# The convolution's last step moved into the slots of the last two attention units

## The chip, the cores and the metric

The kernel runs on one core of one Trainium2 chip. The metric is the device time of one execution in microseconds. The kernel before took 1053.49 us, the median of three runs (1046.73 to 1053.63).

## The reference

Two sequence mixers run over the same input `u` (2048 rows, 448 columns), and a gate per row joins them.

```
g = sigmoid((u * gate_w).sum(-1))
K = 2 * real(einsum("dn,dnl->dl", C, exp(A * dt * l)))     # a kernel of 2048 taps for each column
a = irfft(rfft(u, 4096) * rfft(K, 4096))[:2048] + u * D_skip
q, k, v = u @ wq, u @ wk, u @ wv                            # 16 heads of 28, 4 segments of 512 rows
for s in range(4):
    a_dot = causal_softmax(qs @ ks.T * 28**-0.5) @ vs
    a_mem = phi(qs) @ M / (phi(qs) @ z + 1e-6)              # memory of the segments before
    o     = sigmoid(beta) * a_mem + (1 - sigmoid(beta)) * a_dot
    M, z  = M + phi(ks).T @ vs, z + phi(ks).sum()
b = concat(o) @ wo
out = g * a + (1 - g) * b
```

## The kernel before

The first part, to about 560 us, projects q, k, v, transforms `u` for the convolution and builds the taps; it leaves its results in DRAM. The change is in the second part, `second_half`.

That part goes through 16 attention units: `i = 4 * segment + head group`, four heads in each. A unit has six slots (`r`). In a slot stand one step of the row maxima two units ahead (`maxima`), one step of this unit's scores and exponentials (`weigh`), and, spread between, steps of two other chains: the convolution `cv` (`convolve`: 82 steps, `RATIO` = 1.1 of them a slot from unit 1 on) and the ends of segments (`ends`). The product with the values of a unit (`values`) follows in slot 1 of the next unit.

`seg_end(s)` ends a segment. `norm` takes the denominators out of `pvs` through DRAM (tile `dn`), inverts them, brings them back as `r8` (`r` in the trace), spreads them over the partitions with a matmul by `sel`, and scales `pvs`. Then four output tiles follow: `out_mm` multiplies by `wo`, `store` adds the skip term `u * D_skip * g` and writes the tile to the DRAM buffer `TB`. Then `recall(s + 1)` loads the memory's numerators `am`, inverts their denominators and scales them. Each of these uses the one PSUM buffer `ps_m`; scores, convolution and last step share three buffers `ps_a`.

The convolution's spectrum goes to the DRAM buffer `BB`. When `cv` has ended, with unit 13, its SBUF pool is closed and `finish` begins. It has eight column groups `wc`, each of 64 x 2 x 2 rows of the output. `load` fetches a group of `BB` (tile `bt`), `early` and `late` fetch the group of `TB` (tile `rest`), and `last` makes the inverse transform with four matmuls, multiplies it by the gate and adds it to `rest` on DVE, and stores the result. The rows of a group are spread over the whole sequence, so each group needs rows of all segments: `early` brings the rows of segments 0 to 2 (48 of 64 partitions of each half), `late` those of segment 3.

Segment 3 is ended by `norm(3, 0, 3)` for three head groups and `last_end` for the fourth: it writes four tiles to `TB`, and only then `late` and all eight `last` can run:

```
    k.last_end()
    load_b(6)
    for wc in range(8):
        late(wc)
    for wc in range(8):
        last(wc)
        if wc == 0:
            load_b(7)
```

Engines run their instructions in program order, as a scheduler in the building step put them; so a DMA that waits for a buffer holds up every DMA behind it on the same queue (SP's, ACT's or POOL's). A DMA queue's semaphores are reused after eight issues.

Of the kernel before, what the change touches and what calls it, by code (L numbers as in the profile page):

```python
# [22 lines left out]
D = 448  # L23
# [395 lines left out]
class Feed:  # L419
# [146 lines left out]
def finish(nc, k, fp):  # L566


    bv = k.BB.rearrange("k r (h w) d -> h (k r) w d", h=2)
    ov = k.out.rearrange("(n h w) d -> h n w d", h=2, w=16)  # L570
    tv = k.TB.rearrange("(n h w) d -> h n w d", h=2, w=16)
    bts, rest = {}, {}

    def load(wc):
        for h in range(2):
            bts[wc, h] = fp.tile([128, 2, D], F32, tag="bt", name="bt", bufs=14)
            k.dma(bts[wc, h], bv[h, :, 2 * wc : 2 * wc + 2])

    def early(wc):

        rest[wc] = k.spare(wc)
        for h in range(2):
            k.dma(rest[wc][64 * h : 64 * h + 48], tv[h, :48, 2 * wc : 2 * wc + 2])

    def late(wc):
        for h in range(2):
            k.adma(rest[wc][64 * h + 48 : 64 * h + 64], tv[h, 48:, 2 * wc : 2 * wc + 2])

    def last(wc):
        ws = slice(2 * wc, 2 * wc + 2)  # L590
        py = k.ps("a")
        for w in range(2):
            for h in range(2):
                k.mm(
                    py[64 * h : 64 * h + 64, w, :D], k.fc, bts[wc, h][:, w],
                    start=True, stop=True, tile_position=(0, 64 * h),
                )
        yo = rest[wc]
        for w in range(2):
            i = 2 * wc + w  # L600
            nc.vector.scalar_tensor_tensor(yo[:, w], py[:, w, :D], k.gt2[:, i : i + 1], yo[:, w], ALU.mult, ALU.add)
        for h in range(2):
            k.dma(ov[h, :, ws], yo[64 * h : 64 * h + 64])

    return load, early, late, last

# [198 lines left out]
def attend(nc, k, ap):  # L805
# [177 lines left out]
    def store(s, t, po, xt):  # L983
        i = 4 * s + t
        tb = ap.tile([128, D], F32, tag="tb", name="tb", bufs=2)
        nc.scalar.activation(tb, po, AF.Copy, scale=k.ogt[:, i : i + 1])  # L986
        v.scalar_tensor_tensor(tb, xt, k.gt[:, i : i + 1], tb, ALU.mult, ALU.add)
        (k.adma if s == 3 else k.dma)(k.TB[128 * i : 128 * i + 128], tb)

    def out_mm(s, t, po, hgs):  # L990
        for hg in hgs:
# [4 lines left out]

    def seg_end(s):
        yield from norm(s, 0, 4, k.pdma)
        for t in range(4):
            xt = skip(s, t)  # L1000
            po = k.ps("m")
            out_mm(s, t, po[:, :D], range(4))
            store(s, t, po[:, :D], xt)
            yield
        yield from recall(s + 1)

    def last_end():

        s = 3
        end = norm(s, 3, 4, k.adma)  # L1010
        next(end)
        xts = [skip(s, t) for t in range(4)]
        pos = [k.ps("a") for _ in range(2)]
        for t in range(4):
            out_mm(s, t, pos[t // 2][:, t % 2, :D], range(3))
        for _ in end:
            pass
        for t in range(4):
            po = pos[t // 2][:, t % 2, :D]
            out_mm(s, t, po, [3])  # L1020
            store(s, t, po, xts[t])

    def spare(wc):

        t = ap.tile([128, 2, SEG], F32R, tag="qk"[wc % 2], name="rest", bufs=4)
        return t[:, :, :D].bitcast(F32)

    k.load, k.maxima, k.weigh, k.values, k.seg_end = load, maxima, weigh, values, seg_end
    k.norm, k.last_end, k.spare = norm, last_end, spare


def second_half(nc, k, ap, tp, fp, fin):

    none = object()

    def step(g):
        return next(g, none) is not none

    nothing = iter(())
    attend(nc, k, ap)
    k.load(0)
# [12 lines left out]
    nc.vector.tensor_copy(g16, pm[:16, :128])  # L1056
    k.dma(k.GD.rearrange("(i p) -> i p", p=128), g16)
    k.gt2 = ap.tile([128, 16], F32, name="gt2")
    for h in range(2):
        k.dma(k.gt2[64 * h : 64 * h + 64], k.GD.rearrange("(n h w) -> h n w", h=2, w=16)[h])  # L1060
    fp = fp()
    cv = convolve(nc, k, fp)
    for r in range(3):
        step(ms[1])
    step(ms[0])
    step(ms[0])
    for r in range(3):
        step(ms[1])
    ends = []
    acc = 0.0  # L1070
    vals = nothing
    fi = None
    n = 0
    for i in range(16):
        k.load(i + 3)
        ahead = ms.get(i + 2, nothing)
        behind = ms.get(i + 1, nothing)
        w = k.weigh(i)
        for r in range(6):
            step(ahead)  # L1080
            step(w)
            if r == 0:
                step(behind)
            if r == 1:
                step(vals)
                step(behind)
                if i % 4 == 0 and i > 0:
                    ends.append(k.seg_end(i // 4 - 1))
                if i == 15:
                    ends.append(k.norm(3, 0, 3, k.pdma))  # L1090
            elif ends and not step(ends[0]):
                ends.pop(0)
                if ends:
                    step(ends[0])
            if i >= 1 and fi is None:
                acc += RATIO
# [38 lines left out]
def gated_mix(ctx, tc, k):  # L1135
# [172 lines left out]
```

## Time and profile before

| | before |
|---|---|
| time, median of 3 runs | 1053.49 us (1046.73 to 1053.63) |
| the profiled execution | 1054.63 us, span 1052.8 us |
| mean granted TensorE clock | 0.818 |
| PE busy | 793.4 us (75%) |
| DVE, ACT, POOL busy | 558.5, 559.0, 160.6 us |
| DMA | 151.35 MB, mean 144 GB/s |

The span is the time from the first instruction to the last in one execution that the hardware profiler recorded. PE is TensorE, PEld its weight loads, DVE VectorE, ACT ScalarE, POOL GpSimd; SPq, ACTq and POOLq are DMA issues on the queue of that engine. A row of the timeline has the start, the time it takes, engine, line, operation, output and inputs, count, and in brackets the idle time before it with what ended it. The chain of work that ended last has the start, the duration and what the time went to. In a fp32 product each matmul of the program is two or more records.

### The profile page before, as it was taken

The numbers are of one execution on the slowest core, as the hardware profiler recorded it, in microseconds if no ns is written. First come the engines' busy times: TensorE is split into PE (matmuls) and PEld (weight loads), VectorE is DVE, ScalarE is ACT, GpSimd is POOL, SyncE is SP. The second block draws the span as 40 slices with busy tenths as digits, with TensorE's granted clock in tenths as the row PEclk, the third lists the DMA queues.
The fourth block names the chain that finished last, engine by engine and source line by source line (L and its number), as shares of the span: only waits on it lengthen the run. The fifth ranks groups of instructions, "written<-read, shape, count | busy, mean of one in ns | idle before, by whom it ended". The sixth has DMA issues, their size and how long they took to land.

```text
span 1052.8 us, 18763 instructions
## 1 busy us (share of the span) xinstructions
PE 793.4 (75%) x7413; PEld 440.2 (42%) x7413; DVE 558.5 (53%) x1115; ACT 559.0 (53%) x669; POOL 160.6 (15%) x215
## 2 busy tenths in 40 slices
PE   1265677798777798759975268998999899987485
PEld 0152434355444565437642134444444444444231
DVE  6491524346666476775664045555557555571133
ACT  3425556668888688888883123454335344432210
POOL 0401010101111110101110101113122213222300
PEclk9775776779888899879996565798799789888687
DMA  7853252534222234210624944357446555318607
GB/s 203 247 157 97 83 166 74 167 110 142 82 91 91 90 122 137 86 59 28 190 79 150 348 186 152 96 170 232 131 137 215 177 179 189 127 45 330 137 29 218
DMA packets 90858, 151.35 MB, mean 144 GB/s; under 512 B 20619, under 2 KB 60931, under 8 KB 90723
## 3 DMA queue, kind: packets, MB, share of 16 engines
q1 hardware_dynamic: 80818, 130.26, 39.3%
q10 hardware_dynamic: 8480, 18.62, 4.8%
q0 software_dynamic: 1472, 1.27, 0.5%
q8 instruction: 58, 0.95, 0.4%
q14 instruction: 30, 0.24, 0.1%
HBM read 89.95 MB, written 59.78 MB: 142 GB/s over the span
## 4 chain that ended last, share of the span: by engine, by line
PE 45%; DVE 17%; DMA 14%; ACT 12%; issue 7%; SPq 2%; POOL 1%; DVEq 0%; ACTq 0%; POOLq 0%
PE ps_m L1146 18%; PE ps_a L1146 17%; ACT cs L1139 4%; PE ps_pv L1146 4%; DVE jk L851 4%; DVE X L361 4%; PE ps_arg L1146 3%; DVE Y L365 2%; PE ps_k L1146 2%; PE ps_m L1149 2%; DVE Y L366 2%; DMA dm<-DM 2%; ACT EX L1139 2%; DMA dn<-pvs 2%; ACT L1139 1%
## 5 line engine op out<-in xcount | busy, mean ns | idle before, releaser
L851 DVE CUSTOM_DVE_ANT_0 jk<-ps_a,mk 128x512 f32<-128x512 f32 (+3 forms) x256 | 125.0, 488 | 55.1 <-PE ps_a L1146 47.9
L882 ACT ACTIVATE PT<-ps_a 128x1024 f32<-128x1024 f32 (+1 forms) x96 | 84.1, 881 | 94.7 <-PE ps_a L1146 91.3
L327 POOL TENSOR_TENSOR EX<-EX,cab 128x1024 f32<-128x1024 f32 x28 | 53.5, 1912 | 436.0 <-ACT EX L1139 436.0
L1139 ACT ACTIVATE cs<-ps_arg 128x1024 f32<-128x1024 f32 x112 | 108.3, 1020 | 17.2 <-PE ps_arg L1146 15.4
L1146 PE MATMUL ps_m<-xh,w 112*128 112x512 f32 x256 | 101.7, 443 | 11.4 <-DMA w<-WD 7.5
L1146 PE MATMUL ps_k<-Y,X 128*32 128x64 f32 x3584 | 72.1, 242 | 38.8 <-DVE Y L366 38.4
L1146 PE MATMUL ps_a<-qu,ku 32*128 32x384 f32 (+3 forms) x768 | 90.2, 360 | 6.1 <-DVE mx L851 4.7
L361 DVE TENSOR_TENSOR X<-EX,cs 128x1024 f32<-128x1024 f32 x56 | 68.5, 1223 | 40.1 <-ACT cs L1139 28.6
L1146 PEld LDWEIGHTS ps_k<-Y,X 128*32 128x32 f32 x3584 | 62.1, 124 | 60.2 <-DVE Y L366 48.3
L1146 PEld LDWEIGHTS ps_a<-qu,ku 32*128 32x128 f32 x768 | 69.6, 213 | 17.0 <-DVE mx L851 8.8
L1139 ACT ACTIVATE EY<-ps_arg 128x1024 f32<-128x1024 f32 x56 | 56.4, 1029 | 33.9 <-PE ps_arg L1146 33.7
L893 POOL TENSOR_SCALAR_AFFINE_SELECT PT<-PT 128x256 f32<-128x256 f32 (+1 forms) x96 | 46.5, 488 | 165.4 <-ACT PT L882 163.4
L1146 PE MATMUL ps_a<-ku,qu 32*128 32x512 f32 (+3 forms) x256 | 53.8, 464 | 22.9 <-DVE mx L851 21.8
L1146 PEld LDWEIGHTS ps_m<-xh,w 112*128 112x128 f32 x256 | 51.9, 203 | 40.2 <-issue 14.4
L365 DVE TENSOR_TENSOR Y<-EY,cs 128x1024 f32<-128x1024 f32 x56 | 68.3, 1220 | 0.0
L1139 ACT ACTIVATE cs<-cs,bhp 128x1024 f32<-128x1024 f32 x56 | 64.4, 1150 | 1.8
L1146 PEld LDWEIGHTS ps_a<-ku,qu 32*128 32x128 f32 x256 | 25.6, 216 | 89.4 <-DVE mx L851 44.6
L367 DVE SCALAR_TENSOR_TENSOR Y<-EY,cs 128x512 f32<-128x512 f32 x56 | 38.5, 689 | 39.5 <-ACT cs L1139 39.4
L1146 PE MATMUL ps_arg<-ct,lh 48*128 48x512 bf16 x224 | 48.1, 426 | 9.1 <-ACT cs L1139 7.0
L1146 PE MATMUL ps_m<-xl,w 112*128 112x512 f32 x128 | 53.6, 418 | 0.0
L1146 PEld LDWEIGHTS <-lh 48*128 48x128 bf16 x392 | 21.6, 98 | 70.0 <-issue 46.8
L1146 PE MATMUL ps_m<-wo,pvs 128*128 128x448 f32 x96 | 45.6, 625 | 5.9 <-ACT tb L986 4.9
(182 smaller groups left out, 1350.2 us busy)
## 6 DMA issues: line engine op xcount, KB each, us to landing
w<-WD SPq DMA_DIRECT2D x32, 448.0 KB
qu<-QD SPq DMA_DIRECT2D x16, 512.0 KB
ku<-KD SPq DMA_DIRECT2D x16, 512.0 KB
GU<-gs SPq DMA_DIRECT2D x32, 224.0 KB
GK<-gs ACTq DMA_DIRECT2D x8, 896.0 KB
gk<-GK SPq DMA_DIRECT2D x32, 224.0 KB
gu<-GU SPq DMA_DIRECT2D x32, 224.0 KB
BB<-bs ACTq DMA_DIRECT2D x16, 448.0 KB
```

The lines of the kernel that those rows point to most:

```text
L327: nc.gpsimd.tensor_tensor(o, o, cab, ALU.mult)
L361: v.tensor_tensor(X, ex, t[:, :, 0], ALU.mult)
L365: v.tensor_tensor(Y[:, :, :, :32], lo, y[:, :, :, ::-1], ALU.mult)
L366: v.tensor_tensor(Y[:, 0, :, 32:], ey[:, :, 32:], y[:, 0], ALU.mult)
L367: v.scalar_tensor_tensor(Y[:, 1, :, 32:], ey[:, :, 32:], -1.0, y[:, 1], ALU.mult, ALU.mult)
L851: v.tensor_tensor_reduce(junk[:, :n], pt[:, x, o : o + n], k.mk[:, SEG - n :], 1.0, -3e38, ALU.add, ALU.max, mx[:, 3 - t, h : h + 1],)
L882: nc.scalar.activation(PT[:, 2 * hp : 2 * hp + 2, 512 * b : 512 * b + n], pt[:, :, :n], AF.Exp, scale=SCALE)
L893: nc.gpsimd.affine_select(sl, sl, pat, ALU.is_ge, 0.0, base=0, channel_multiplier=-1)
L1139: return tc.keep_in_program_order(nc.scalar.activation(*args, **kw))
L1146: tc.keep_in_program_order(nc.tensor.matmul(*args, **kw))
L1149: tc.keep_in_program_order(nc.tensor.transpose(*args))
```

## The change

- `cv` ends with unit 12: its ratio goes from 1.1 to 1.15 steps a slot. `finish` begins there.
- The segment ends get on faster: a step in slot 0 and slots 2 to 5 as before, but in unit 13 two steps in every slot; and the first steps of `recall` go along with the output tiles. Segment 2 thus ends within unit 13.
- `skip_last`, in slot 2 of unit 11, writes the skip term of segment 3 (`u * D_skip * g`) to `TB`, so that `TB` is complete without the attention of segment 3.
- `load` fetches both halves of a group in one DMA (four buffers of 896 KB instead of fourteen of 448 KB); `join` replaces `early` and `late` and fetches the rows of all four segments in two DMAs of 64 partitions, into six buffers.
- `last` runs in slots: groups 0 to 3 in slots 2 to 5 of unit 14, groups 4 to 7 in slots 0 to 3 of unit 15. It stores the rows of segments 0 to 2 to the output, and those of segment 3 to a new DRAM buffer `YD`.
- `last_end` loads the four tiles of `YD`, adds `(1 - g)` times its attention output in one DVE instruction a tile, and writes segment 3 to the output, alternately on SP's and ACT's queue.

```diff
 def finish(nc, k, fp):
-    bv = k.BB.rearrange("k r (h w) d -> h (k r) w d", h=2)
+    bv = k.BB.rearrange("k r (h w) d -> (k r) h w d", h=2)
     ov = k.out.rearrange("(n h w) d -> h n w d", h=2, w=16)
     tv = k.TB.rearrange("(n h w) d -> h n w d", h=2, w=16)
+    yv = k.YD.rearrange("(n h w) d -> h n w d", h=2, w=16)
     def load(wc):
-        for h in range(2):
-            bts[wc, h] = fp.tile([128, 2, D], F32, tag="bt", name="bt", bufs=14)
-            k.dma(bts[wc, h], bv[h, :, 2 * wc : 2 * wc + 2])
-    def early(wc):
-        rest[wc] = k.spare(wc)
-        for h in range(2):
-            k.dma(rest[wc][64 * h : 64 * h + 48], tv[h, :48, 2 * wc : 2 * wc + 2])
-    def late(wc):
-        for h in range(2):
-            k.adma(rest[wc][64 * h + 48 : 64 * h + 64], tv[h, 48:, 2 * wc : 2 * wc + 2])
+        bts[wc] = fp.tile([128, 2, 2, D], F32, tag="bt", name="bt", bufs=4)
+        k.dma(bts[wc], bv[:, :, 2 * wc : 2 * wc + 2])
+    def join(wc):
+        rest[wc] = fp.tile([128, 2, D], F32, tag="rest", name="rest", bufs=6)
+        for h in range(2):
+            k.dma(rest[wc][64 * h : 64 * h + 64], tv[h, :, 2 * wc : 2 * wc + 2])
     def last(wc):
...
-                    py[64 * h : 64 * h + 64, w, :D], k.fc, bts[wc, h][:, w],
+                    py[64 * h : 64 * h + 64, w, :D], k.fc, bts[wc][:, h, w],
...
         for h in range(2):
-            k.dma(ov[h, :, ws], yo[64 * h : 64 * h + 64])
+            k.dma(yv[h, :, ws], yo[64 * h + 48 : 64 * h + 64])
+        for h in range(2):
+            k.dma(ov[h, :48, ws], yo[64 * h : 64 * h + 48])
 def attend(nc, k, ap):
...
-        (k.adma if s == 3 else k.dma)(k.TB[128 * i : 128 * i + 128], tb)
+        k.dma(k.TB[128 * i : 128 * i + 128], tb)
+    def skip_last():
+        for t in range(4):
+            xt = skip(3, t)
+            i = 12 + t
+            v.tensor_scalar(xt, xt, k.gt[:, i : i + 1], None, ALU.mult)
+            k.dma(k.TB[128 * i : 128 * i + 128], xt)
     def seg_end(s):
         yield from norm(s, 0, 4, k.pdma)
+        memory = recall(s + 1)
         for t in range(4):
...
+            next(memory)
             yield
-        yield from recall(s + 1)
+        yield from memory
     def last_end():
...
-        xts = [skip(s, t) for t in range(4)]
+        yds = []
+        for t in range(4):
+            yd = ap.tile([128, D], F32, tag="xt", name="yd", bufs=4)
+            k.dma(yd, k.YD[128 * t : 128 * t + 128])
+            yds.append(yd)
...
         for t in range(4):
-            po = pos[t // 2][:, t % 2, :D]
+            po, yd, i = pos[t // 2][:, t % 2, :D], yds[t], 12 + t
             out_mm(s, t, po, [3])
-            store(s, t, po, xts[t])
+            v.scalar_tensor_tensor(yd, po, k.ogt[:, i : i + 1], yd, ALU.mult, ALU.add)
+            (k.dma, k.adma)[t % 2](k.out[128 * i : 128 * i + 128], yd)
 def second_half(nc, k, ap, tp, fp, fin):
...
-            elif ends and not step(ends[0]):
-                ends.pop(0)
-                if ends:
-                    step(ends[0])
-            if i >= 1 and fi is None:
+            if r != 1 or i == 13:
+                for _ in range(2 if i == 13 else 1):
+                    while ends and not step(ends[0]):
+                        ends.pop(0)
+            if 1 <= i <= 12:
                 acc += RATIO
...
-            if fi is not None and r % 2 == 1:
-                load_b(n)
+            if i == 11 and r == 2:
+                k.skip_last()
+            if i == 13 and r < 4:
+                load_b(r)
+            if i == 14 and r >= 2 or i == 15 and r < 4:
+                last(n)
+                if n < 2:
+                    join(n + 6)
+                if n < 4:
+                    load_b(n + 4)
                 n += 1
...
-        if i == 13:
+        if i == 12:
             for _ in cv:
                 pass
-            fi = fin()
-            load_b, early, late, last = finish(nc, k, fi)
-        if i == 14:
+            load_b, join, last = finish(nc, k, fin())
+        if i == 13:
             for wc in range(6):
-                early(wc)
+                join(wc)
...
-    early(6)
-    early(7)
     step(vals)
     k.last_end()
-    load_b(6)
-    for wc in range(8):
-        late(wc)
-    for wc in range(8):
-        last(wc)
-        if wc == 0:
-            load_b(7)
-RATIO = 1.1
+RATIO = 1.15
...
+    k.YD = dr.tile([SEG, D], F32, name="YD")
```

More of the change, by code (lines that the diff above doesn't have):

```diff
@@ L594, in last @@
                 k.mm(
-                    py[64 * h : 64 * h + 64, w, :D], k.fc, bts[wc, h][:, w],
+                    py[64 * h : 64 * h + 64, w, :D], k.fc, bts[wc][:, h, w],
                     start=True, stop=True, tile_position=(0, 64 * h),
                 )
-        yo = rest[wc]
+        yo = rest.pop(wc)
         for w in range(2):
@@ L602, in last @@
         for h in range(2):
-            k.dma(ov[h, :, ws], yo[64 * h : 64 * h + 64])
-    return load, early, late, last
+            k.dma(yv[h, :, ws], yo[64 * h + 48 : 64 * h + 64])
+        for h in range(2):
+            k.dma(ov[h, :48, ws], yo[64 * h : 64 * h + 48])
+    return load, join, last
 def project(nc, k, pp):
@@ L1018, in last_end @@
         for t in range(4):
-            po = pos[t // 2][:, t % 2, :D]
+            po, yd, i = pos[t // 2][:, t % 2, :D], yds[t], 12 + t
             out_mm(s, t, po, [3])
-            store(s, t, po, xts[t])
-    def spare(wc):
-        t = ap.tile([128, 2, SEG], F32R, tag="qk"[wc % 2], name="rest", bufs=4)
-        return t[:, :, :D].bitcast(F32)
+            v.scalar_tensor_tensor(yd, po, k.ogt[:, i : i + 1], yd, ALU.mult, ALU.add)
+            (k.dma, k.adma)[t % 2](k.out[128 * i : 128 * i + 128], yd)
     k.load, k.maxima, k.weigh, k.values, k.seg_end = load, maxima, weigh, values, seg_end
-    k.norm, k.last_end, k.spare = norm, last_end, spare
+    k.norm, k.last_end, k.skip_last = norm, last_end, skip_last
 def second_half(nc, k, ap, tp, fp, fin):
@@ L1071, in second_half @@
     vals = nothing
-    fi = None
     n = 0
```

## The prediction

> **What bounds the kernel now.** I read the page first, then the busy time by stage, then the chain of work that ended last.
>
> ```profile
> span 1052.8 us, 18763 instructions
> PE 793.4 (75%) x7413; PEld 440.2 (42%) x7413; DVE 558.5 (53%) x1115; ACT 559.0 (53%) x669; POOL 160.6 (15%) x215
> 820.00:917.00 97.00, 90.86 (x566) 43.81 (x566) 56.46 (x166) 42.24 (x53) 22.20 (x40) 0.86 0.51 168
> 944.00:971.00 27.00, 19.98 (x115) 10.08 (x111) 7.26 (x21) 9.30 (x12) 4.60 (x10) 0.90 0.90 331
> 971.00:1002.00 31.00, 15.75 (x107) 8.37 (x107) 8.17 (x13) 7.20 (x10) 12.06 (x18) 0.67 0.56 123
> 1002.00:1034.00 32.00, 24.31 (x90) 9.40 (x90) 7.29 (x13) 3.13 (x5) 0.00 (x0) 0.87 0.22 68
> 1034.00:1053.00 19.00, 10.66 (x40) 3.87 (x40) 9.49 (x16) 0.00 (x0) 0.00 (x0) 0.68 0.74 227
> ```
>
> The columns behind the stretch are its length and the busy time of PE, weight loads, DVE, ACT and POOL, then granted clock, DMA share and GB/s. While the convolution lasts (820 to 917) PE works 90.86 of 97 us and is the bound; moving work among those units buys nothing. From 944 on it is not: PE idles 7.0, 15.3, 7.7 and 8.3 us in the four stretches. The change acts there. I call the values product of unit i pv(i); pv(12) to pv(15) divide the tail into pieces. Rows of the timeline and of the chain:
>
> ```profile
> 936.06 2.29 PE ps_pv L1146 x32
> 941.05 1.72 PE L1146 MATMUL ps_a<-pr,cb 128*64 128x448 f32 x8
> 957.65 2.36 PE L1146 MATMUL ps_pv<-PT,V 128*32 128x512 f32 x32
> 978.86 2.36 PE L1146 MATMUL ps_pv<-PT,V 128*32 128x512 f32 x32
> 1002.65 4.28 PE ps_pv L1146 x32
> 1006.93 9.22 PE ps_a L1146 x24
> 1016.14 0.44 PE ps_m L1146
> 1016.67 0.76 DVE pvs L970
> 1017.46 0.70 DVE pvs L972
> 1018.20 1.03 PE ps_a L1146 x2
> 1026.55 0.33 ACTq L988 DMA_DIRECT2D TB<-tb  x1
> 1030.87 9.49 ACTq L587 DMA_DIRECT2D rest<-TB  x16
> 1034.84 10.66 PE L1146 MATMUL ps_a<-bt,fc 128*64 128x448 f32 x40 [5.45 <-issue]
> 1045.55 1.28 DVE L601 SCALAR_TENSOR_TENSOR rest<-ps_a,gt,rest 128x448 f32<-128x448 f32 x2 [0.23 <-PE ps_a L1146]
> ```
>
> From pv(15) to the end pass 1052.8 - 1002.65 = 50.15 us. Up to 1018.20 that is attention; then four output tiles go to TB (last store issued at 1026.55), come back (first `late` load at 1030.87), and 40 of the 64 matmul records of `last` run behind that return.
>
> **The change, piece by piece.**
>
> *From pv(15) to the end.* The head of this piece stays: 4.28 + 9.22 + 0.44 + 0.76 + 0.70 with small gaps is 15.55 us, to the first hg 3 product. Then per tile there is one product (1.03) and one DVE addition, with no ACT copy and no return from TB. The order of the changed program shows tiles 1 and 3 still waiting until their neighbour in the same PSUM tile is read, now by DVE. The addition has the shape of L601 below, 0.68: 1.03 + 0.76 (0.68 and two gaps of 0.04) + 1.03 + 1.03 + 0.76 + 1.03 + 0.72 = 6.4. The last output store then needs 0.33 to issue and must land. Nearest rows: an `xt` load of the same 224 KB took 2.60; the TB store issued at 1026.55 let its reader go at 1030.87, that is 4.0 after its issue, with the last bt loads beside it. Nothing lies beside the new store, so I take 2.6 (bounds 2.6 and 4.0). With 0.5 to close, the piece is 15.55 + 6.4 + 0.33 + 2.6 + 0.5 = 25.4 us instead of 50.15: **24.8 us less**.
>
> ```profile
> 978.61 2.60 DMA xt<-in_A_u
> L601 DVE SCALAR_TENSOR_TENSOR rest<-ps_a,gt,rest 128x448 f32<-128x448 f32 x16 | 10.0, 678 | 10.3 <-DMA rest<-TB 6.9 <-PE ps_a L1146 3.3
> L1146 PE MATMUL ps_a<-bt,fc 128*64 128x448 f32 x64 | 15.4, 643 | 5.5 <-issue 5.5
> 953.54 3.27 PE L1146 MATMUL ps_m<-wo,pvs 128*128 128x448 f32 x8
> 971.05 5.67 PE L1146 MATMUL ps_m<-wo,pvs 128*128 128x448 f32 x8 [4.85 <-ACT tb L986]
> 982.06 0.45 PE L1146 MATMUL ps_m<-r,sel 8*128 8x512 f32 x1
> 983.35 0.49 PE L1146 MATMUL ps_m<-r,sel 8*128 8x512 f32 x1 [0.49 <-DVE am L948]
> ```
>
> ```profile
> 912.60 2.33 PE ps_pv L1146 x32
> 946.51 3.02 SPq L577 DMA_DIRECT2D bt<-BB  x6
> ```
>
> *Until pv(12).* The convolution has 82 steps. Until unit 12 has ended the old ratio makes 72 x 1.1 = 79.2 of them, the new one all 82. So only the last back transform (1.72, up to 3.3 at the low clock) crosses pv(12): +2.5, pv(12) at **938.5**.
>
> *pv(12) to pv(13).* Before 957.65 - 936.06 = 21.6. Out goes the back transform (1.7) and one selection product (0.5), in come output tiles 2 and 3 of segment 2 (3.27 each, 6.5) and the four recall products. Those show 982.06 to 983.35, 1.3 a piece, as PE and DVE take turns over one `ps_m` buffer; with other matmuls between them I take 3 us for the four (bounds 1.9, their PE time, and 5.2). 21.6 - 2.2 + 6.5 + 3 = 28.9; pv(13) at **967.4**.
>
> *pv(13) to pv(14).* Before 978.86 - 957.65 = 21.2, of which two tiles took 3.27 and 5.67, and 4.85 was the wait in front of the second. That leaves 7.4 of attention. Into it come `last` 0 to 4. One `last` is 15.4 / 8 = 1.93 (eight of 64 records), five are 9.6. 17.0; pv(14) at **984.4**. The wait of 4.85 was for a TB store that queued behind bt:
>
> ```profile
> 950.37 10.10 DMA bt<-BB
> 960.53 9.76 DMA TB<-tb
> 984.34 5.71 DMA dn<-pvs
> 991.80 0.79 PE L1146 MATMUL ps_m<-r,sel 8*128 8x512 f32 x1 [6.50 <-DVE am L948]
> 995.99 2.51 DMA r<-RD
> 998.63 0.76 PE L1146 MATMUL ps_m<-r,sel 8*128 8x512 f32 x1 [6.03 <-DMA r<-RD]
> ```
>
> In the changed SP order four bt loads (3.7 MB) and am stand ahead of these stores. Before, bt began at 946.51, behind a last back transform at 941.05; now that transform stands ahead of pv(12), about 934, so bt begins about 940. At the 331 GB/s of that stretch the backlog is through near 955, before tile 2 needs its tb buffer at about 957. So I count no wait here; if the stores are as late as before, it is 4.85 again.
>
> *pv(14) to pv(15).* Before 23.8 us, and not PE time: the denominators of unit 14 leave by dn, come back inverted by r, and PE stands 6.50 and 6.03 us. The chain is the same after the change. `last` 5 to 7 (5.8) and the rest of the unit's scores lie under it, in those 12.5 us, and cost nothing; without that cover they would cost 5.8. I take 23.8; pv(15) at **1008.2**.
>
> *What else is issued.* `skip_last` moves four POOL products (no more, no fewer) to unit 11 and adds four DVE scalings there. No scaling of that shape is in the trace; it lies between 0.18 (the cast below) and L601's 0.68, so at most 2.7 us, on a DVE that is busy 56 of 97 us. Its four stores and the reloads behind them can hold SP for 4 x 2.6 = 10 us. The convolution's loads behind them run three columns ahead: 82 steps for 32 columns are 2.6 a column, at 1.15 a slot and a sixth of a unit (936.06 - 912.60 = 23.5 us) a slot, so 26 us of cover; I take nothing, and 10 without it. On SP's queue the tail has 67 issues instead of 57 (16 YD stores and 4 YD loads added, ACT's 20 TB issues gone); at 0.33 that is 22 us spread over 65. The first YD load waits for the stores of `last` 7, about 1003, 15 us before its data is added. A wait is added in front of bt 6 and bt 7: the `rest` loads 6 and 7 reuse buffers (six of them) and stand on SP until the outputs of `last` 0 and 1 have landed, with YD, out and bt issues queued behind them. I have bt 7 landing at 991 to 996, and `last` 7 wanting it at 994.
>
> ```profile
> 990.66 0.19 DVE L923 CAST rs<-rc 128x48 fp32r<-128x48 f32 x1
> qu<-mn POOLq DMA_DIRECT2D x16, 16.0 KB, 2.5
> ```
>
> The smallest transfers with a landing time here, 16 KB, take 2.5 us from issue to landing; a YD store has 56 KB, and 16 of them in a row would be 40 us, but up to eight are in flight.
> The Trainium skill, "DMA: Bandwidth & Descriptors", "Rules for kernel authors", speaks against such stores: under 64 KB one pays mostly overhead; its fixed cost is about 2.0 us, an estimate of 32 us for the 16 if each were waited for. No run here shows a YD store yet.
>
> *Sum.* -24.8 + (1008.2 - 1002.65 = 5.6) = -19.2: a span of 1033.6. Around its span the profiled execution of 1054.63 had 1.8 us, and it stands 1.1 above the median of 1053.49, so the median should be **1034**. Of the bounds, the lower ones (recall -1.1, a warm pv(15) -2, dn -1.7, both under A) lead to 1029; of the upper ones (recall +2.2, TB wait +4.85, SP +10, uncovered `last` +5.8, landing +1.4) any one of the larger leads to 1039 to 1044.
>
> **The rivals.** A measurement here tells about 1% (10.5 us, 1043 or 1064) from no change.
>
> *A, faster still, near 1025.* The products of `last` fill the gaps of 971 to 1002, where the granted clock was 0.67, and it stays near 0.87. pv(15) then takes 2.36 and not 4.28 (2 us), `last` 1.58 instead of 1.93, by the row below (2.8 over eight), dn lands in 4.0 as in the other units (1.7), and the recall products hide (3): 9.5 less. For it: the gaps are where the work goes. Against: the wait for r outlasts `last` 7, so one gap stays right before pv(15).
> The Trainium skill, "TensorE: Matmul & The Clock Gate", "Part 1: The HAM clock gate", has the clock halve after an idle window of some 3.4 us; the gaps of 6.50 and 6.03 and the 0.67 agree, and by that rule the remaining gap keeps pv(15) slow.
>
> ```profile
> 1024.66 4.73 PE L1146 MATMUL ps_a<-bt,fc 128*64 128x448 f32 x24
> 917.38 3.98 DMA dn<-pvs
> ```
>
> *B, the unit before takes the gain, near 1044.* Unit 13 now puts twelve uses of the single `ps_m` buffer into one unit. If tiles 2 and 3 go at 5.67 instead of 3.27 (+4.8) and the TB store is late again (+4.85), everything behind is 9.7 later. For it: exactly that happened at 971. Against: bt starts some 6 us earlier.
>
> *C, slower, near 1075.* SP becomes the bound in units 14 and 15. A round there is two additions (1.36), four issues (1.3), a landing (4.0) and a bt load at its 10.10: 16.8. Were bt 4 to 7 to go in such rounds one after the other from the end of `last` 0 (975), bt 7 would land at 1042, and with `last` 7 (1.9) and three selections (1.6 each) pv(15) stands at 1049, the end at 1075. Two rounds, for the two reused buffers, give 1041. It decides once bt 7 lands after 1002, and the kernel gets slower than before from about 1022. Against: bt 4 and 5 have no landing to wait for, and that 10.10 was fourteen loads deep.
>
> **How the numbers follow.** Forecast 0.58, A 0.15, B 0.15, C 0.12 (half of it the two-round form at 1041). Faster by over 1%: forecast and A, and 0.05 of B and the milder C: 0.78. Slower: 0.08, the harder C (0.06) and an edge of B. Within 1%: the rest of B and C, 0.14. The range, 1022 to 1050, holds the forecast, A, B and two-round C, less their edges.
>
> **What would show it.** Right: pv(15) near 1008 and some 25 us from there to the end; no TB load behind the last output tile; `last` 5 to 7 in front of the wait for r. Wrong: pv(13) past 972 with PE waiting for ACT tb (B); PE waiting for bt at `last` 6 or 7 (C); pv(14) to pv(15) well over 24 us; DVE or SP stalls in unit 11 from the scaled xt; YD arriving after the last products.

## The result, and the profile after

The changed kernel takes 1038.87 us (median of 12 runs, 1027.41 to 1051.58) where the kernel before takes 1048.43 us beside it (12 runs, 1043.77 to 1055.64). The ratio is 0.9873, 95% interval 0.9835 to 0.9911: 1.3% faster. The forecast of 1034 was 1.8% below 1053.49, so by this ratio some two thirds of the forecast gain came. The experiments below show that even this agreement has another cause than the one I gave: the large piece of the forecast came true to within a microsecond and was given back elsewhere, and a gain that I had ruled out took its place.

The ratio leaves out executions that are more than 1.5% above their kernel's fastest, five of the changed kernel's twelve and its profiled one (1046.95 us, mean granted clock 0.83) among them, and over all twelve the medians stand at 0.991; so below stages are compared rather than totals, with two more profiles of the same kernel beside. First its page, then busy time by stage, with the columns as in the prediction.

```profile
span 1045.2 us, 18770 instructions
PE 789.2 (76%) x7413; PEld 440.5 (42%) x7413; DVE 560.5 (54%) x1119; ACT 556.6 (53%) x665; POOL 161.2 (15%) x215
```

```profile
720.00:820.00 100.00, 87.55 (x574) 42.57 (x570) 58.62 (x173) 42.97 (x53) 24.11 (x41) 0.93 0.54 172
820.00:917.00 97.00, 82.91 (x536) 39.24 (x536) 54.36 (x150) 39.17 (x49) 25.19 (x40) 0.91 0.50 164
917.00:944.00 27.00, 18.67 (x116) 9.43 (x114) 13.21 (x43) 7.64 (x10) 6.63 (x13) 0.62 0.40 139
944.00:971.00 27.00, 21.21 (x81) 11.99 (x83) 11.58 (x31) 5.76 (x9) 2.59 (x5) 0.85 0.42 152
971.00:1002.00 31.00, 25.69 (x200) 12.15 (x199) 10.59 (x19) 10.53 (x13) 7.42 (x15) 0.89 0.97 267
1002.00:1034.00 32.00, 25.65 (x100) 10.85 (x96) 8.35 (x17) 2.71 (x4) 2.89 (x5) 0.70 0.40 122
```

The gap that the forecast meant to fill is filled: from 971 to 1002 PE works 25.69 us instead of 15.75. New is the idle PE from 917 to 944 (18.67 instead of 23.05 us, the clock 0.62 instead of 0.81), and from 820 to 917 (82.91 instead of 90.86).

The PE timeline of the changed kernel, with the marks pv(12) to pv(15) and the places where time is lost (L1153 is the helper that records every matmul):

```profile
871.59 6.34 PE L1153 MATMUL ps_m<-wo,pvs 128*128 128x448 f32 x8 [6.89 <-DVE mn L861]
880.11 3.27 PE L1153 MATMUL ps_m<-wo,pvs 128*128 128x448 f32 x8
925.19 0.58 PE L1153 MATMUL ps_a<-ku,qu 32*128 32x256 f32 x2 [3.52 <-DVE mx L850]
929.26 0.58 PE L1153 MATMUL ps_a<-ku,qu 32*128 32x256 f32 x2 [2.85 <-DVE pr L535]
939.53 3.89 PE L1153 MATMUL ps_pv<-PT,V 128*32 128x512 f32 x32
955.13 3.27 PE L1153 MATMUL ps_m<-wo,pvs 128*128 128x448 f32 x8 [0.72 <-ACT tb L985]
963.63 3.27 PE L1153 MATMUL ps_m<-wo,pvs 128*128 128x448 f32 x8 [0.72 <-ACT tb L985]
967.63 0.49 PE L1153 MATMUL ps_m<-r,sel 8*128 8x512 f32 x1 [0.72 <-ACT tb L985]
972.16 0.79 PE L1153 MATMUL ps_m<-r,sel 8*128 8x512 f32 x1 [0.41 <-DVE am L947]
974.54 3.45 PE L1153 MATMUL ps_pv<-PT,V 128*32 128x512 f32 x32
979.47 1.72 PE L1153 MATMUL ps_a<-bt,fc 128*64 128x448 f32 x8
991.63 2.36 PE L1153 MATMUL ps_pv<-PT,V 128*32 128x512 f32 x32
1001.56 3.25 PE L1153 MATMUL ps_a<-bt,fc 128*64 128x448 f32 x8 [4.90 <-DMA bt<-BB]
1015.18 0.79 PE L1153 MATMUL ps_m<-r,sel 8*128 8x512 f32 x1 [4.44 <-DMA r<-RD]
1019.15 4.50 PE L1153 MATMUL ps_pv<-PT,V 128*32 128x512 f32 x32
1023.58 9.77 PE L1153 MATMUL ps_a<-wo,pvs 128*128 128x448 f32 x24
1035.40 1.02 PE L1153 MATMUL ps_a<-wo,pvs 128*128 128x448 f32 x2 [1.63 <-DVE pvs L971]
```

The last row of DVE's timeline is the last addition; from its end the output store has 3.7 us to land until the span closes.

```profile
1040.80 0.68 DVE L1035 SCALAR_TENSOR_TENSOR yd<-ps_a,ogt,yd 128x448 f32<-128x448 f32 x1 [1.11 <-PE ps_a L1153]
```

**A ruler for comparing kernels.** The part ahead of the second half is the same in all kernels here, but begins its last stage, the copies `gs` on ACT (L489), anywhere from 562.7 to 574.2 us. So the pieces are counted from the first `gs` copy. The rows of line 489 of the kernel before, of the changed kernel, and of two experiments (`before_r115` and `own_xt_b`), in this order, give its start behind the minimum, median and maximum of one copy:

```profile
L489 ACT ACTIVATE gs<-ps_a x16: 912/917/918, 567.9 to 625.4; 128x896 f32<-128x896 f32 x16
```

```profile
L489 ACT ACTIVATE gs<-ps_a x16: 911/917/917, 572.2 to 623.8; 128x896 f32<-128x896 f32 x16
```

```profile
L489 ACT ACTIVATE gs<-ps_a x16: 912/917/917, 573.0 to 628.3; 128x896 f32<-128x896 f32 x16
```

```profile
L489 ACT ACTIVATE gs<-ps_a x16: 912/914/917, 568.6 to 630.4; 128x896 f32<-128x896 f32 x16
```

The table has the distances between the PE starts of the values products in the profiled executions (so it has the spread of single executions, up to 4.0 us in a column for the three of the changed kernel). `after`, `after_b` and `after_c` are the changed kernel three times; the others are the experiments.

| us | gs to pv(9) | to pv(10) | to pv(12) | to pv(13) | to pv(14) | to pv(15) | to the end | gs to the end |
|---|---|---|---|---|---|---|---|---|
| before | 299.9 | 23.7 | 44.5 | 21.7 | 21.2 | 23.7 | 50.2 | 484.9 |
| after | 286.6 | 36.0 | 44.8 | 35.0 | 17.1 | 27.5 | 26.1 | 473.0 |
| after_b | 283.7 | 34.4 | 40.8 | 35.2 | 17.1 | 29.2 | 26.8 | 467.1 |
| after_c | 282.9 | 37.0 | 43.4 | 35.4 | 17.2 | 28.0 | 25.9 | 469.8 |
| before_r115 | 292.5 | 23.9 | 42.4 | 22.3 | 13.9 | 23.6 | 50.5 | 469.1 |
| before_ends | 290.5 | 25.2 | 39.6 | 21.7 | 25.9 | 20.8 | 51.7 | 475.4 |
| before_skip | 301.9 | 32.1 | 45.9 | 22.2 | 21.0 | 24.1 | 50.1 | 497.4 |
| own_xt_b | 293.4 | 25.2 | 44.6 | 35.6 | 17.2 | 27.8 | 26.0 | 469.7 |
| rest8 | 285.2 | 36.2 | 44.8 | 34.9 | 20.4 | 21.8 | 27.6 | 470.7 |
| no_last | 283.6 | 34.3 | 42.1 | 33.1 | 13.0 | 21.9 | 26.4 | 454.4 |
| late_last | 287.0 | 34.3 | 40.7 | 35.3 | 12.6 | 18.4 | 58.6 | 487.0 |

From before to after: -13.3, +12.3, +0.3, +13.3, -4.1, +3.8, -24.1. The tail gives what was forecast; units 10 and 13 take it back; the units up to 9 give what nobody asked of them.

### The profile page after: what moved, and what is told of

The parts are those of the page before. It is cut to its first block, busy times and chain, and to the rows that moved or that the text cites. A ratio compares the mean times of both kernels' runs of the same rounds, so it can differ in the third digit from the quotient of the medians.

```text
span 1045.2 us, 18770 instructions
## 1 busy us (share of the span) xinstructions
PE 789.2 (76%) x7413; PEld 440.5 (42%) x7413; DVE 560.5 (54%) x1119; ACT 556.6 (53%) x665; POOL 161.2 (15%) x215
## 4 chain that ended last, share of the span: by engine, by line
PE 47%; DVE 18%; DMA 13%; ACT 13%; issue 6%; SPq 2%; POOL 1%; DVEq 0%; ACTq 0%; POOLq 0%
PE ps_m L1153 20%; PE ps_a L1153 15%; ACT cs L1146 4%; DVE jk L850 4%; PE ps_pv L1153 4%; PE ps_arg L1153 4%; DVE X L361 3%; PE ps_k L1153 2%; DVE Y L365 2%; DMA qu<-QD 2%; PE ps_m L1156 2%; DVE Y L366 2%; ACT EX L1146 2%; DMA dn<-pvs 2%; DMA dm<-DM 2%
## 5 line engine op out<-in xcount | busy, mean ns | idle before, releaser
L1153 PE MATMUL ps_m<-xh,w 112*128 112x512 f32 x256 | 104.9, 457 | 11.1 <-DMA w<-WD 7.3
L1153 PE MATMUL ps_k<-Y,X 128*32 128x64 f32 x3584 | 74.7, 247 | 37.3 <-DVE Y L366 37.0
L1153 PE MATMUL ps_a<-qu,ku 32*128 32x512 f32 (+3 forms) x768 | 91.5, 364 | 3.7 <-DVE mx L850 2.9
L361 DVE TENSOR_TENSOR X<-EX,cs 128x1024 f32<-128x1024 f32 x56 | 68.3, 1220 | 40.7 <-ACT cs L1146 29.0
L1153 PEld LDWEIGHTS ps_k<-Y,X 128*32 128x32 f32 x3584 | 64.5, 127 | 59.4 <-DVE Y L366 46.8
L1153 PEld LDWEIGHTS ps_a<-qu,ku 32*128 32x128 f32 x768 | 70.8, 215 | 18.5 <-issue 6.5
L1153 PE MATMUL ps_a<-ku,qu 32*128 32x128 f32 (+3 forms) x256 | 53.6, 456 | 29.3 <-DVE mx L850 25.8
L1153 PEld LDWEIGHTS ps_m<-xh,w 112*128 112x128 f32 x256 | 53.9, 210 | 40.7 <-issue 14.8
L1153 PEld LDWEIGHTS ps_a<-ku,qu 32*128 32x128 f32 x256 | 25.7, 214 | 86.8 <-DVE mx L850 50.6
L1153 PE MATMUL ps_m<-xl,w 112*128 112x512 f32 x128 | 55.3, 432 | 0.0
L1153 PE MATMUL ps_arg<-ct,lh 48*128 48x512 bf16 x224 | 48.2, 427 | 9.1 <-ACT cs L1146 7.0
L1153 PEld LDWEIGHTS <-lh 48*128 48x128 bf16 x392 | 21.7, 99 | 71.5 <-issue 48.4
L1153 PE MATMUL ps_m<-wo,pvs 128*128 128x448 f32 x96 | 44.1, 607 | 8.3 <-DVE mn L861 6.9
```

The lines of the kernel that those rows point to most:

```text
L361: v.tensor_tensor(X, ex, t[:, :, 0], ALU.mult)
L1153: tc.keep_in_program_order(nc.tensor.matmul(*args, **kw))
```

## The experiments

Each ratio is against the kernel before, beside it on the same chip, with its 95% interval. "Theory 1" and "theory 2" are those of the quoted expectation.

**1. `before_skip`: the cost of the scaled skip term.** The kernel before, with `skip_last` added in the same slot, its result written to a buffer that nobody reads.

```diff
+            if i == 11 and r == 2:
+                k.skip_last()          # stores to YD instead of TB
```

> The kernel before with one part of the change alone and to no use: skip_last in slot 2 of unit 11, with its four loads, four POOL products, four DVE scalings and four stores, which go to an unused DRAM buffer; all else as before. Theory 1 (the scalings wait in DVE's order for tiles whose loads wait for buffers): 5 to 10 us slower, ratio 1.005 to 1.010, with PE waiting for DVE mn in units 9 to 11. Rival (they cost their own time on a DVE that is 56% busy): within 1 us, 1.000.

Measured: 1.0081 (1.0043 to 1.0118). Theory 1 holds: unit 10 takes 32.1 us instead of 23.7. In the waits of this kernel between 855 and 905 PE waits for the short DVE instruction `mn`, a wait that the kernel before does not have:

```profile
PE ps_m L1155 <- DVE mn L862: 5.1, 1, 5.1
```

The changed kernel has the same, larger. Its waits from 855 to 900, then its chain, then DVE's timeline:

```profile
POOL xt L979 <- DMA xt<-in_A_u: 28.5, 7, 11.5
DVE xt L994 <- POOL xt L979: 13.7, 4, 6.7
PE ps_m L1153 <- DVE mn L861: 6.9, 1, 6.9
```

```profile
861.37 1.91 DMA TB<-xt
864.68 4.51 DMA xt<-in_A_u
869.36 1.11 POOL xt L979
870.86 0.68 DVE mn L861
```

```profile
867.30 0.57 DVE L994 TENSOR_SCALAR xt<-xt,gt 128x448 f32<-128x448 f32 x1 [4.01 <-POOL xt L979]
870.49 0.45 DVE L994 TENSOR_SCALAR xt<-xt,gt 128x448 f32<-128x448 f32 x1 [2.63 <-POOL xt L979]
```

Read from the bottom: a scaling waits on DVE for POOL, POOL for the load of `xt`, and that load for its buffer, which comes free when the store `TB<-xt` of an earlier tile has landed. `mn`, 0.68 us long and needed by PE, stands behind the scaling in DVE's order. The Trainium skill, "PSUM — Partial Sum Buffer", "Engine vs sequencer instructions", calls the queues of ScalarE, VectorE and GpSimd strict first in, first out; the two rows at 870.49 and 870.86 agree.

**2. `own_xt` and `own_xt_b`: three buffers of their own for these four tiles.** The changed kernel with

```diff
-            xt = skip(3, t)
+            xt = skip(3, t, "xs", 3)   # a tag of its own, three buffers
```

> The changed kernel with one difference: the four skip tiles of skip_last get three buffers of their own instead of the four of the segment ends, so their loads need not wait for older tiles and the four DVE scalings no longer stand waiting in DVE's order in front of mn. Theory 1 (the scalings wait for late loads, and PE waits 6.9 us for the mn queued behind them in unit 10 and then runs 3 us longer at a low clock): that wait is gone, the distance from the pvs copy of unit 9 to that of unit 10 falls from 36.0 us to about 25, and the ratio to the kernel before falls from 0.987 to about 0.978 (1025 us). Rival (unit 10 was a chance dip of the clock, the scalings cost only their own time): no change, 0.987.

> The changed kernel with three buffers of their own for the four tiles of the scaled skip term, once more, beside the changed kernel on the same chip. Theory 1 (the 11 us that its trace shows saved in unit 10 reach the end): 1.0% below the changed kernel of this call. Theory 2 (the time given back: the later waits for bt and r and a lower clock take it): within 0.4% of it.

> The changed kernel once more, beside the next one on the same chip. 0.983 to 0.991 as in its other comparisons.

Measured: 0.985 (0.9795 to 0.9905) and 0.9868 (0.9826 to 0.9909); the changed kernel beside the second, 0.9886 (0.984 to 0.9932). In the trace unit 10 is back at 25.2 us and the wait for `mn` is gone, some 12 us less than in `after_c`. The time does not show it (the first expectation's 0.978 did not come), and the table says where it went: the stretch up to pv(9) is 293.4 instead of 282.9. With buffers free from the start, the scheduler put these tiles at the beginning of the second half (scalings at 605 to 615 us), and there they hold up `gs`. PE's waits between 560 and 650, `after_c` and then `own_xt_b`, the latter with a wait of ACT for a load of `xt` that `after_c` does not have:

```profile
PE ps_a L1153 <- ACT gs L489: 22.0, 5, 13.5
```

```profile
PE ps_a L1153 <- ACT gs L489: 28.5, 5, 13.6
ACT gs L489 <- DMA xt<-in_A_u: 15.0, 1, 15.0
```

6.5 us of the 10.5 stand in the two rows of PE. From `gs` to the end both take the same, 469.8 and 469.7. Theory 2's result came, for a reason in neither theory: the price of `skip_last` moved with its instructions.

**3. `before_r115`: the new ratio alone.** The kernel before with one number changed.

```diff
-RATIO = 1.1
+RATIO = 1.15
```

> The kernel before with the convolution at 1.15 steps a slot instead of 1.1, nothing else. Theory 1 (the denser ratio alone brings the 9 us that the changed kernel was ahead by unit 9, since more convolution between the attention's steps leaves PE fewer short gaps and a higher granted clock): ratio 0.990 to 0.995, units 0 to 9 in about 205 us instead of 212, granted clock from 720 to 820 about 0.92. Theory 2 (the ratio moves the same PE work earlier and no more; the clock stays 0.86): ratio 0.998 to 1.004, units 0 to 9 in 210 to 213 us.

Measured: 0.9861 (0.981 to 0.9913), median 1041.56 beside 1041.73 of the changed kernel in the same call. Theory 1 holds in sign, and its 0.990 to 0.995 meets the interval at the upper edge: one number brings as much time as the whole change. 15.8 us are gained from `gs` to the end (484.9 to 469.1), nearly all in two pieces: 7.4 up to pv(9), 7.3 from pv(13) to pv(14). The second has a mechanism that its PE and SP timelines show:

```profile
931.84 3.35 PE L1146 MATMUL ps_pv<-PT,V 128*32 128x512 f32 x32
954.10 2.36 PE L1146 MATMUL ps_pv<-PT,V 128*32 128x512 f32 x32
962.59 3.27 PE L1146 MATMUL ps_m<-wo,pvs 128*128 128x448 f32 x8
967.99 2.36 PE L1146 MATMUL ps_pv<-PT,V 128*32 128x512 f32 x32
```

```profile
931.74 10.12 SPq L577 DMA_DIRECT2D bt<-BB  x14
950.64 0.32 SPq L988 DMA_DIRECT2D TB<-tb  x1
```

With the convolution over before pv(12), the `bt` loads go out at 931.74 instead of 946.51. The share of the DMA engines falls to 0.05 from 957 to 964, where the kernel before still has 0.86 from 965 to 971; and the tile at 962.59 follows without a wait where the kernel before waited 4.85 us and then ran at 5.67. The 7.4 us up to pv(9) are almost all in units 1 to 3 (pv(0) to pv(3): 653.56 to 715.34 before, 656.40 to 711.63 here, 6.6 us less); from pv(3) to pv(9) nothing is gained (152.4 and 153.9). The busy time from pv(0) to pv(3) says how, first of the kernel before (with a part of that stretch below it), then of the ratio alone:

```profile
653.56:715.34 61.78, 58.42 (x391) 27.82 (x389) 32.81 (x105) 28.79 (x35) 10.35 (x21) 0.82 0.42 131
665.30:679.00 13.70, 13.59 (x56) 5.82 (x58) 6.52 (x18) 4.26 (x6) 2.09 (x4) 0.50 0.44 145
```

```profile
656.40:711.63 55.23, 51.33 (x395) 25.25 (x393) 33.42 (x106) 29.78 (x36) 10.35 (x21) 0.96 0.52 162
```

The work is the same (391 and 395 records), and PE needs 51.33 us for it instead of 58.42, at a granted clock of 0.96 instead of 0.82. The clock of the kernel before is 0.50 for 13.7 us from 665.30; with the ratio alone it is 1.00 from 660.8 to pv(3). This is no chance of one execution: in the fourteen profiles, the ten at 1.15 take 54.4 to 58.2 us for these units at a clock of 0.91 to 0.98, the four at 1.1 take 59.1 to 61.8 at 0.82 to 0.88. Theory 1 is right about the clock, but had put the gain into 720 to 820, where both have 0.86, and its reason (fewer short gaps) is not borne out: PE is idle for 3.4 us of the stretch before and for 3.9 with the ratio alone, and its longest single wait there is 0.7 and 0.6 us. Why the clock rises is not settled.

**4. `ratio11`: all of the change but the ratio.**

```diff
-RATIO = 1.15
+RATIO = 1.1
```

> The changed kernel with the old ratio of 1.1 convolution steps a slot; the three or so steps that are left are done at the end of unit 12. Theory 1 (the ratio only shifts some three steps, 3 us of work, among units): 0.987, within 0.003, and the values copies of units 1 to 9 at the same distances as in the changed kernel. Rival (the 9 us which the changed kernel has gained up to unit 9, with a clock of 0.91 to 0.93 against 0.82 to 0.86, come from the denser convolution): those units go back to the distances of the kernel before, 0.995.

Measured: 0.995 (0.9909 to 0.9992), the number of the rival, although the profiled execution (1038.5, its shortest of twelve) is as short as the changed kernel from `gs` to pv(9) (286.5 us). Most of that lies ahead of pv(0), though, and pv(0) to pv(3) takes 59.1 us, as the rival wanted. The other eleven executions ran at a granted clock of 0.811 to 0.829. Times decide, so with experiment 3 there is a square:

| | last step behind the attention | last step in the slots, with all that belongs to it |
|---|---|---|
| ratio 1.1 | 1 | 0.995 (0.9909 to 0.9992) |
| ratio 1.15 | 0.9861 (0.981 to 0.9913) | 0.9873, 0.9831, 0.9886 |

Moving the last step is worth half a per cent at the old ratio (its interval all but reaches 1) and nothing that can be told at the new one.

**5. `before_ends`: the new schedule of the segment ends alone.**

```diff
-            elif ends and not step(ends[0]):
-                ends.pop(0)
-                if ends:
-                    step(ends[0])
+            if r != 1:
+                while ends and not step(ends[0]):
+                    ends.pop(0)
...
+        memory = recall(s + 1)         # a step of it behind each output tile
```

> The kernel before with the changed schedule of the segment ends alone: one step in slots 0 and 2 to 5, and the recall's steps along with the output tiles; ratio 1.1, last step behind the attention as before. Theory 1 (the ends schedule brings the gain of the middle units): 0.990 to 0.995, the units 4 to 9 about 6 us shorter, and units 1 to 3 as before. Theory 2 (it brings nothing by itself; the units 1 to 3, in which no segment end stands, were ahead too): 0.998 to 1.004.

Measured: 0.9967 (0.9933 to 1.0), between the two. Theory 1's place is wrong: pv(3) to pv(9) takes 152.7 us as before (152.4). The trace's 9.4 us up to pv(9) lie ahead of pv(0) for the most part (from `gs`, 77.8 instead of 85.7), where no segment end stands; so an edit there shifts work far from it, as the scheduler orders the program anew. The other profiles bear this out: from `gs` to pv(0) the three kernels with the old schedule of the ends take 83.4 to 86.8 us, the eight profiles with the new one 76.7 to 79.8, and the three with `xt` buffers of their own 85.9 to 89.9 again.

**6. `no_last`: what the inverse transform still costs.** No `bt` loads, no products, no additions in `last`; the stores stay.

```diff
     def load(wc):
-        bts[wc] = fp.tile(...); k.dma(bts[wc], ...)
+        pass
     def last(wc):
-        py = k.ps("a"); (four products); (two additions)
```

> The changed kernel without the convolution's last step itself: no bt loads, no matmuls and no DVE additions in last, rest goes to the output and to YD as it is; all its other loads and stores stay. It leaves out 64 matmul records (16.9 us of PE in the changed kernel's trace). Theory 1 (five of the eight are paid in full in front of the values product of unit 14, the other three lie under the wait for r, but for 4.9 us of waiting for bt 6): 9 to 10 us for the five and 4 for the wait, ratio about 0.974. Rival 2 (all of it lies in idle time of PE): at most 4 us less, 0.983. Rival 3 (all of it is paid, 17 to 22 us): 0.967 or lower.

Measured: 0.9751 (0.9699 to 0.9803), as theory 1 had it: some 12 us of the last step are still paid. The table puts 9.7 of them into the last two units (13.0 + 21.9 against 17.1 + 27.5). Unit 13 stays long (33.1 against 35.0 to 35.4), so at most some 2 us of its length have to do with the last step.

**7. `rest8`: no wait for a `rest` buffer.** Eight buffers instead of six, all loads ahead of the outputs.

```diff
-        rest[wc] = fp.tile(..., bufs=6)
+        rest[wc] = fp.tile(..., bufs=8)
...
-            for wc in range(6):
+            for wc in range(8):
                 join(wc)
```

> The changed kernel with eight rest buffers instead of six, all filled at the end of unit 13: no load on SP's queue waits for the outputs of last 0 and 1 any more. Theory 1 (that wait holds up the issue of bt 6, and PE stands 4.9 us in front of last 6): bt 6 is issued some 4 us earlier, PE does not wait for it, the values product of unit 15 comes 4 us after that of the changed kernel less 4, and the ratio is about 0.983. Rival (the transfers are at their full rate there, DMA share 0.97, so an earlier issue only queues): bt 6 lands as late as before, 0.987.

Measured: 0.9856 (0.9806 to 0.9906), not to be told from the changed kernel, so the time does not decide between the two. In the changed kernel bt 6 was issued only at 994.43, behind a `rest` load that waited for an output to land, and arrived 6.99 us later (its chain):

```profile
994.43 6.99 DMA bt<-BB
```

Without that wait pv(14) to pv(15) falls from 27.5 to 21.8, but the loads ahead now delay bt 4 (10.28 us from its issue to landing), pv(13) to pv(14) grows from 17.1 to 20.4, and the wait for `r` grows to 6.21. PE's timeline of `rest8`:

```profile
987.82 1.72 PE L1151 MATMUL ps_a<-bt,fc 128*64 128x448 f32 x8 [3.27 <-DMA bt<-BB]
1008.16 0.79 PE L1151 MATMUL ps_m<-r,sel 8*128 8x512 f32 x1 [6.21 <-DMA r<-RD]
```

Both pieces together: 44.6, 46.3 and 45.2 in the three profiles of the changed kernel, 42.2 here.

**8. `late_last`: the eight `last` behind the attention loop, ahead of `last_end`.**

```diff
-            if i == 14 and r >= 2 or i == 15 and r < 4:
-                last(n) ...
...
     step(vals)
+    for n in range(8):
+        last(n) ...
     k.last_end()
```

> The changed kernel with the eight last steps behind the attention loop (after the values product of unit 15 is issued) instead of in the slots of units 14 and 15; all else, skip_last and YD included, stays. Theory 1 (five of them are paid in the slots, three are covered by the wait for r): pv(15) 9 to 13 us earlier than in the changed kernel, and up to 15 us of PE work more behind it, less what covers the last denominators' way (9 us): 2 us slower than the changed kernel or no difference, ratio 0.987 to 0.992. Rival (the slots are what brings the gain, and without them the kernel is back where it was): 12 us slower than the changed kernel, 0.998.

Measured: 1.0024 (0.9987 to 1.006). Theory 1 fell; the rival has the sign, and the loss is larger than its 12 us (medians 1052.89 and, for the changed kernel beside it, 1032.27). The products take 30 us (997 to 1027) for 16.8 us of PE's time, because four buffers of `bt` let only four loads run ahead:

```profile
1013.24 3.25 PE L1152 MATMUL ps_a<-bt,fc 128*64 128x448 f32 x8 [6.72 <-DMA bt<-BB]
1022.13 5.10 PE L1152 MATMUL ps_a<-bt,fc 128*64 128x448 f32 x16 [5.63 <-DMA bt<-BB]
```

So the slots hide the transfers as well as PE's time.

**9. `after_b`: the changed kernel once more, for the ratio's run beside it.**

> The changed kernel once more, unchanged, on the chip of the three that follow, so that they can be compared with it and not only with the kernel before. The ratio to the kernel before should lie in 0.983 to 0.991 as before.

Measured: 0.9831 (0.9779 to 0.9883).

**10. `best`: everything that the traces suggested by then.** Own `xt` buffers, seven `rest` buffers, and the first part of segment 3's norm already in unit 14, for two head groups.

```diff
-                if i == 15:
-                    ends.append(k.norm(3, 0, 3, k.pdma))
+                if i == 14:
+                    ends.append(k.norm(3, 0, 2, k.pdma))
```

> The changed kernel with three repairs: skip_last's tiles have three buffers of their own; seven rest buffers, and the load of the eighth group stands behind bt 6 on SP's queue; and the denominators of segment 3 go in two halves, head groups 0 and 1 from unit 14 on, 2 and 3 behind unit 15, so that no wait for r stands in front of the values product of unit 15. Theory 1: 10 us from the wait in unit 10, some 10 us from the wait for r and its three selections, less 4 to 6 us for the longer products and selections at the end, 2 us from bt: 1020 us where the changed kernel takes 1039, ratio about 0.968. Rival (the last stretch is bound by its transfers, DMA share 0.97, so the wait only moves): 0.977 with skip_last's repair alone.

Measured: 0.987 (0.9813 to 0.9928), no better than the changed kernel; neither 0.968 nor the rival's 0.977 came. The wait for `r` did not go, it came earlier, ahead of pv(14), and a second one stands at the end:

```profile
983.50 0.79 PE L1153 MATMUL ps_m<-r,sel 8*128 8x512 f32 x1 [8.29 <-DMA r<-RD]
1011.89 0.79 PE L1153 MATMUL ps_m<-r,sel 8*128 8x512 f32 x1 [4.44 <-DMA r<-RD]
```

## Why the prediction was right, and where it was wrong

The time lay in the range, 5 us above the forecast. That it came so close was in part luck: errors of 12 to 13 us each way cancelled. Step by step:

**pv(15) to the end: right.** 25.4 forecast; 26.1, 26.8 and 25.9 in the three profiles. The single DVE addition per tile, the waits within a PSUM pair and no return from `TB` came as described; the landing took 3.4 as summed and 3.7 as measured.

**pv(13) to pv(14): right, and so was its reason.** 17.0 forecast, 17.1 measured: `last` went at 1.72, and nothing waited for a `TB` store, because `bt` starts earlier. But `before_r115` shows that this wait goes with the earlier end of the convolution alone (13.9 there, without any `last`), so its 4.85 us are no gain of the moved step.

**"Moving work among those units buys nothing": wrong.** This was the step that mattered most. I read 90.86 busy of 97 us as a bound that only less work could lower. From 720 to 820 the changed kernel has PE busy for 87.55 us instead of 93.06, with nearly the same count of records (574 and 578), at a clock of 0.93 instead of 0.86. The row of the kernel before:

```profile
720.00:820.00 100.00, 93.06 (x578) 44.85 (x580) 55.73 (x163) 42.47 (x53) 23.99 (x42) 0.86 0.52 167
```

So the busy time of PE is not a fixed quantity: one product takes longer at a lower granted clock, as pv(14) with 2.36 us and pv(15) with 4.50 (the clock 0.50 there) show. 13.3 us were gained up to pv(9), and the ratio alone is worth 1.4% in time.

**`skip_last` at nothing: wrong by some 11 us.** Unit 10 went from 23.7 to 36.0 us, and to 25.2 without the wait (`own_xt_b`). I priced four scalings on a DVE with spare time and 10 us of SP. Neither was the cost; what stood behind a scaling in DVE's order was. The sign that I had named, a stall of DVE from the scaled `xt`, came, one unit earlier than I had it. The busy share of DVE (56 of 97 us) said nothing on that, and I had not asked what is queued behind the instruction if its load is late.

**Until pv(12): the right number by luck, 938.5 against 939.5, from two errors that cancel**, the two above, and an execution whose `gs` began 4.3 us later.

**pv(12) to pv(13): 28.9 forecast, 35.0 measured.** Most of the 6.1 lies behind the second output tile. From its end at 958.40 to pv(13) pass 16.1 us, where my terms give 10.4 (two tiles of 3.27, 3 for the recall, 0.85 of scores as before). The four recall products took 967.63 to 972.95, 5.3 us where I took 3 (the upper bound, 5.2): 2.3. The single `ps_m` had to be emptied ahead of tile 3 and of the recall, 0.72 each: 1.4. The other 2.0 are scores that stand between these rows. pv(12) itself ran at 3.89 instead of 2.29, but up to the second tile's end the piece is only 0.3 longer than my terms. pv(12) is slow behind the waits of 3.52 and 2.85 (925.19 and 929.26), and 917 to 944 has the clock at 0.62; `before_r115`, whose convolution ends as early, has 0.63 there. This is rival B's place and its first sign (pv(13) past 972 with waits for ACT `tb`), though not its mechanism: the tiles behind the first two took 3.27 each and the late store did not come.

**pv(14) to pv(15): 23.8 forecast, 27.5 measured.** Not unchanged: `last` 6 waited 4.90 for bt 6, rival C's two-round form, in the place that I named for it. The addition of `last` 6 then stood ahead of unit 14's reciprocal on DVE, so `r` came late too: the `dn` loads, issued from 994.95 to 996.47, landed 5.3 to 6.6 us after their issue, and the reciprocal began at 1006.04. `rest8` shows that this wait can be moved; in the sum of both units it brought 2.4 to 4.1.

**Rival A: half of it came.** The clock between 971 and 1002 rose from 0.67 to 0.89 as the gaps were filled, but pv(15) still took 4.50 behind the wait of 4.44 for `r`, where pv(14) took 2.36. `before_r115` has the like, 4.19 behind 5.05. The Trainium skill, "TensorE: Matmul & The Clock Gate", "Part 1: The HAM clock gate" (an idle window of about 3.4 us halves the clock), agrees: by it the one gap left keeps pv(15) slow. No such window stood ahead of the half clock at 665.30 in experiment 3.

**The small stores.** `YD` cost no wait that the profile shows: the four `yd` loads are issued from 1013.5 to 1015.3, and the first of their data is read at 1036.46. Whether the stores of 56 KB make the transfers beside them dearer no run separates; the share of 0.97 at 267 GB/s from 971 to 1002, against 0.90 at 331 from 944 to 971 before, is at least not against it. The Trainium skill, "DMA: Bandwidth & Descriptors", "Rules for kernel authors" (under 64 KB mostly overhead), points that way. The prediction's estimate of 32 us for the 16 stores shows nowhere as a wait.

**Where the expected gain went.** Against the ratio alone (`before_r115`, 469.1), the changed kernel (`after_c`, 469.8) has -9.6 up to pv(9), -24.6 in the tail, and +13.1 in unit 10, +1.0, +13.1 in unit 13, +3.3 and +4.4 in the last two. Of the -9.6, 4.1 lie ahead of pv(0), where the new schedule of the ends shows (experiment 5), and 5.6 from pv(3) to pv(9): only the kernels with both that schedule and the ratio of 1.15 have 148.3 to 150.3 us there, the others 150.6 to 154.6. The tail's gain is real and is paid for by three things that the move needs: the skip term ahead of time, a whole segment end within one unit, and the inverse transform in two units with waits of their own. What stays open is why the clock of the units up to 9 is higher, and how much of `ratio11`'s short profiled execution its usual ones have.

## What to carry to other kernels

Run the smallest edit of a change by itself before crediting the large one: here a ratio of 1.15 instead of 1.1 brought as much time as all of it. An instruction put into an engine's order costs not its duration but what stands behind it when its input is late, so look up the next instructions on its queue and who waits for them. A tail that is emptied into earlier units must bring its transfers, its buffers and its preparations along, and each of them is a new wait in a place that had been full.

## What the hardware showed that I had not expected

- After a wait of 6.89 us the eight records of an output tile took 6.34 us (871.59), the same shape 3.27 us 8.5 us later (880.11). Here a wait was paid nearly half again in the products behind it (3.07 us).
- Time goes with the granted clock between executions of one kernel, if not strictly: of its 24 runs here the changed kernel's shortest is 1027.41 us at 0.847, its longest 1051.58 at 0.822.
- An edit of one number moved the granted clock of a stretch from 0.82 to 0.96 (pv(0) to pv(3) in `before_r115`), 7.1 us less of PE for the same work. The clock of the kernel before stood at 0.50 there for 13.7 us, although PE waited for nothing longer than 0.7 us.
